# A fused attention and MLP kernel: its first six chunks of q loaded two tokens to a row, its first 420 operations put in a written order, its end cut over two PSUM banks

## The chip, the core and the metric

The kernel runs on one core of one Trainium2 chip. The metric is the device time of one execution in microseconds (us). Three runs of the kernel before the change took 611.60, 611.12 and 610.27 us; their median is 611.12 us. Engine names are those of the profile: PE is TensorE's matmul side and PEld its weight loads, DVE is VectorE, ACT is ScalarE, POOL is GpSimd, SP is SyncE, which here only issues DMAs. Times "at 37.9" are microseconds from the first instruction of the profiled execution.

## The reference

q, k and v have 4 batches, 8 heads, 768 tokens and a head size of 64. Tokens come in blocks of 64. For each batch and head:

```python
for b in range(nb):
    intra = einsum('bhic,bhjc->bhij', qb, kb) * Dmask         # lam ** (i - j), causal
    intra = einsum('bhij,bhjd->bhid', intra, vb)
    inter = einsum('bhid,bhde->bhie', qb * lam_pow, kv_state)
    out[:, :, sl] = intra + inter
    kv_state = lam_block * kv_state + einsum('bhsd,bhse->bhde', kb * rev_pow, vb)
x = out.transpose(0, 2, 1, 3).reshape(3072, 512)              # tokens x (heads, head size)
h = x @ w_in                                                  # 512 x 2048, float64 weights
return maximum(0.01 * h, h) @ w_out                           # 2048 x 512
```

The weights arrive as 64-bit floats and are turned into 32-bit ones on the chip.

## The kernel before

**Tiling.** A chunk `c` is 128 tokens (two blocks) of one batch, all heads; there are 24 chunks, six to a batch. Four chunks make a group `g` of 512 tokens, so there are six groups. `w_in` and `w_out` are cut into eight parts `p` of 256 hidden columns.

**Precision.** Each operand of the MLP is split in three tiles h, l and m (`xh`, `xl`, `xm` and `wh`, `wl`, `wm`), and a product is three passes of TensorE, h·h, l·l and m·m, in one PSUM bank, with one ACT rescaling (L658) ahead of the m pass.

**A chunk** goes through these steps. `load_kq` (L338) and `load_v` (L388) issue its loads on SP's queue: k and q in two halves of four heads, 128 KB each, v in one piece of 256 KB, all in rows of 64 floats. `transposes` (PE, L403) turns k and q by four 128x128 transposes each; ACT copies the results to SBUF (L414, L415); POOL or DVE scales k in place (L419) and makes the scaled q, `qsT` (L423; DVE for chunks 0 to 3, POOL after that). `scores` (PE, matmuls of 64x64 by `quad`, L313) makes the scores and the state's update, both in the bank `psc`. DVE masks the scores (L452) and adds the update to the state (L457, L459), POOL scales the state (L462). `outputs` (PE, L313) adds the masked scores times v and then, in two halves, the state's part in the bank `po`; between the halves a tiny copy (L491) is waited for. ACT makes `xh` (L507), DVE `xl` (L508) and `xm` (L510). Attention of a chunk needs the state of the chunk before it in the same batch.

**A weight part** `wi` takes two loads of 512 KB in rows of 2 KB (L566), three ACT operations for each half (L578, L580, L582), two DVE operations for each half (L584, L585) and then `wh` (ACT L591 or DVE L593), `wl` (DVE L596) and `wm` (DVE L602).

**Up** (`up(g, p)`, L640) multiplies a weight part with one group: for each of two halves f, four matmuls each of h, l and m, in one of three banks; ACT rescales and applies the leaky ReLU (L658, L661), and SP writes the result to DRAM (L664). From the third group on, **down** reads it back, splits it and multiplies it with `w_out` (L700) into eight accumulators, two for each of four blocks of 128 tokens: one for h and l, one for m.

**Order.** The kernel first records all its operations in a `Plan`, each with its engine (or two to choose from), a cost in us, what it reads and writes, and a rank from its place in the list `seq`. `emit` simulates the engines with these costs, always takes the operation that can start first, and then issues them engine by engine in the order found. Each engine executes its instructions in that order. Where the plan sees PE idle before the first product of the MLP, it puts in dummy transposes of the identity (`busy`, L266); nine more stand at the start (`WARM`).

**The end.** For the last block of 128 tokens, the m passes of the last two parts come last, in two halves of 256 columns of one accumulator in the bank `pt`; each half is then combined by DVE (L729) and written out on SP's queue (L732). After the last operation, PE runs 24 dummy matmuls of strips of the array and eight small ones (`strips`, L802, L809), whose results nobody reads.

## Time and profile before

| what | value |
|---|---|
| runs | 611.60, 611.12, 610.27 us; median 611.12 |
| profiled execution | span 609.73 us from first to last instruction; no other time is listed for it, and the median of the runs is 1.39 us above the span |
| busy | PE 601.4 us (99%), DVE 313.1 (51%), ACT 269.2 (44%), POOL 86.7 (14%) |
| mean granted TensorE clock | 1.000 |
| PE busy in stretches of 5 us from 0 to 40 | 3.14, 4.96, 3.81, 4.25, 3.51, 4.11, 4.53, 4.66 |
| PE busy from 40 to 600 | 559.6 of 560 |
| DVE busy from 15 to 40 | 22.8 of 25 |
| DMA | 105.18 MB, mean 173 GB/s; 180 to 295 GB/s in stretches of 1.5 to 7 us from 2.5 to 30 us |

The profile's page gives busy time as a share of the whole span. Here that says little, because the kernel has stages with different limits: the stretch up to 40 us, in which the loads, the first chunks and the first weights come in, and the rest. A group's "mean ns" is the length of one instruction from start to end; back to back, DVE's operations start 0.08 us closer than that, and PE's matmuls of 512 columns 0.226 us apart, because they overlap in the pipeline.

### The profile page before, as it was taken

To read this page: it belongs to the slowest core of one execution; us is meant where nothing else is said; L and a number is where in the kernel's file an instruction comes from. 1 tells how busy PE (TensorE), PEld (TensorE's weight loads), DVE (VectorE), ACT (ScalarE), POOL (GpSimd) and SP (SyncE) were. 2 spreads that over 40 slices of the span, in tenths; PEclk is the share of its full clock that TensorE was granted. 3 is DMA by queue.
4 is the path that set the end of the run, shared out by engine and by line. 5 is a ranking of instruction groups with operands and counts; after the bars stand their busy time and mean duration, and the time that the engine had idled before them with its cause. 6 is when DMAs were issued, how large, how long until landed. Compare 5 with 4: busy or idle time off the path is not lost.

```text
span 609.7 us, 13012 instructions
## 1 busy us (share of the span) xinstructions
PE 601.4 (99%) x5426; PEld 497.8 (82%) x5426; DVE 313.1 (51%) x418; ACT 269.2 (44%) x430; POOL 86.7 (14%) x90
## 2 busy tenths in 40 slices
PE   7799999999999999999999999999999999999999
PEld 6678888888888888888788888888888888888887
DVE  4999764334244426226366755545454544636531
ACT  4678974444465656555577522222222313214111
POOL 1654422114233004104000000000000000000000
DMA  9899865666888878887685843524334343333201
GB/s 208 219 267 249 239 190 136 167 150 186 190 219 240 217 229 215 214 245 214 226 304 218 284 145 103 173 71 142 133 104 137 108 135 114 130 104 125 82 1 69
DMA packets 147754, 105.18 MB, mean 173 GB/s; under 512 B 123632, under 2 KB 124400, under 8 KB 147696
## 3 DMA queue, kind: packets, MB, share of 16 engines
q1 hardware_dynamic: 147552, 104.36, 58.7%
q8 instruction: 42, 0.69, 0.5%
q14 instruction: 16, 0.13, 0.1%
q10 hardware_dynamic: 144, 0.00, 0.0%
HBM read 68.69 MB, written 35.65 MB: 171 GB/s over the span
## 4 chain that ended last, share of the span: by engine, by line
PE 95%; DVE 4%; DMA 1%; ACT 0%; issue 0%; DVEq 0%; ACTq 0%
PE b L640 43%; PE b L700 18%; PE po L700 11%; PE psc L700 11%; PE po L313 4%; PE pt L700 4%; PE psc L313 4%; DVE w L585 1%; PE pt L403 1%; DMA att<-in_k_dram 1%; DVE w L584 0%; DVE att L452 0%; PE psc L802 0%; DVE att L459 0%; DVE att L423 0%; DVE wm L602 0%
## 5 line engine op out<-in xcount | busy, mean ns | idle before, releaser
L682 ACT ACTIVATE xh<-att 128x1024 fp32r<-128x1024 f32 x48 | 50.8, 1061 | 148.8 <-PE b L700 140.7
L683 DVE SCALAR_TENSOR_TENSOR xl<-att,xh 128x1024 fp32r<-128x1024 f32 x48 | 58.6, 1222 | 97.9 <-ACT xh L682 94.7
L640 PE MATMUL b<-xh,wh 128*128 128x512 f32 (+2 forms) x392 | 103.6, 387 | 1.2 <-ACT xh L507 0.8
L640 PE MATMUL b<-xm,wm 128*128 128x512 f32 (+2 forms) x392 | 104.4, 392 | 0.0
L640 PE MATMUL b<-xl,wl 128*128 128x512 f32 (+2 forms) x392 | 103.3, 387 | 0.0
L640 PEld LDWEIGHTS b<-xh,wh 128*128 128x128 f32 x392 | 72.9, 188 | 16.8 <-ACT xh L507 0.9
L640 PEld LDWEIGHTS b<-xl,wl 128*128 128x128 f32 x392 | 72.8, 188 | 14.8
L640 PEld LDWEIGHTS b<-xm,wm 128*128 128x128 f32 x392 | 71.4, 188 | 15.1 <-ACT b L658 0.3
L658 ACT ACTIVATE b<-b 128x512 f32<-128x512 f32 (+2 forms) x97 | 56.2, 580 | 60.5 <-PE b L640 60.3
L661 ACT ACTIVATE gs<-b 128x512 f32<-128x512 f32 (+2 forms) x97 | 56.9, 593 | 43.6 <-PE b L640 38.5
L700 PE MATMUL b<-wh,xh 128*128 128x512 f32 x192 | 74.7, 389 | 0.0
L700 PE MATMUL b<-wl,xl 128*128 128x512 f32 x192 | 74.7, 389 | 0.0
L685 DVE SCALAR_TENSOR_TENSOR xm<-xl,xh 128x1024 fp32r<-128x1024 f32 x48 | 58.7, 1225 | 4.7
L462 POOL TENSOR_TENSOR att<-att 128x256 f32<-128x256 f32 x40 | 35.0, 876 | 57.6 <-DVE att L459 57.6
L700 PEld LDWEIGHTS b<-wh,xh 128*128 128x128 f32 x192 | 36.0, 188 | 7.5
L700 PEld LDWEIGHTS b<-wl,xl 128*128 128x128 f32 x192 | 36.0, 187 | 7.4
L452 DVE TENSOR_TENSOR att<-psc,att 128x512 f32<-128x512 f32 x24 | 16.5, 689 | 42.6 <-PE psc L313 42.5
L423 POOL TENSOR_TENSOR att<-att 128x512 f32<-128x512 f32 (+1 forms) x20 | 24.5, 1223 | 95.5 <-DVE att L383 46.6
L700 PE MATMUL psc<-wh,xh 128*128 128x512 f32 x96 | 37.3, 389 | 0.0
L700 PE MATMUL psc<-wl,xl 128*128 128x512 f32 x96 | 37.3, 389 | 0.0
L700 PE MATMUL psc<-wm,xm 128*128 128x512 f32 x96 | 37.3, 389 | 0.0
L700 PE MATMUL po<-wh,xh 128*128 128x512 f32 x96 | 37.3, 389 | 0.0
(79 smaller groups left out, 793.0 us busy)
## 6 DMA issues: line engine op xcount, KB each, us to landing
att<-g SPq DMA_DIRECT2D x48, 512.0 KB, 3.3
g<-gs SPq DMA_DIRECT2D x47, 512.0 KB, 4.0
raw<-in_moe_w_in_dram SPq DMA_DIRECT2D x16, 512.0 KB, 5.6
raw<-in_moe_w_out_dram SPq DMA_DIRECT2D x16, 512.0 KB, 5.0
att<-in_k_dram SPq DMA_DIRECT2D x48, 128.0 KB, 4.2
att<-in_v_dram SPq DMA_DIRECT2D x24, 256.0 KB, 4.6
out_dram<-gs SPq DMA_DIRECT2D x23, 256.0 KB, 2.2
wo<-w SPq DMA_DIRECT2D x8, 512.0 KB, 5.9
```

The costliest lines, as they stand in the source:

```text
L313: nc.tensor.matmul(dst[HALF[cols]], lhsT=lhsT[HALF[rows]], rhs=rhs[HALF[rows]], start=start, stop=True, skip_group_check=True)
L403: nc.tensor.transpose(out=at[y], in_=src[:, 2 * y:2 * y + 2, :].rearrange("p a d -> p (a d)"), identity=ident)
L423: add(eng, us, lambda: e.tensor_tensor(o, x, _bc(pow_q, 2, 2)[:, :, m, :], op=ALU.mult), ["fq", dep], [f"qsT{i}"])
L452: add("DVE", 0.69, lambda: nc.vector.tensor_tensor(sc, psc[:, :, lower, :], decay, op=ALU.mult), ["psc", "fk"], ["sc"])
L462: add("POOL", 0.7, lambda new=new, j=j: nc.gpsimd.tensor_tensor(state[(j + 1) % 4], new, _bc(lam_c, 2, D), op=ALU.mult), [f"st{j % 4}", "f ...
L640: nc.tensor.matmul(dst, lhsT=w[z][:, kk * 2 * P + f * P:kk * 2 * P + (f + 1) * P], rhs=x[z][:, kk, toks], start=start and kk == 0, stop=kk ...
L658: add("ACT", ns, lambda b=b: nc.scalar.activation(out=b, in_=b, func=AF.Copy, bias=0.0, scale=S + 1.0), [], [kb], rank=-1.5)
L661: add("ACT", ns, lambda b=b, r=r: nc.scalar.activation(out=r, in_=b, func=AF.Prelu, bias=0.0, scale=1.0 / WS, alpha=0.01), [kb], [f"gs{jg} ...
L682: add("ACT", 1.05, lambda: nc.scalar.activation(out=h, in_=graw[j], func=AF.Copy, bias=0.0, scale=NEAR), reads, wr("h"))
L683: add("DVE", 1.25, lambda: nc.vector.scalar_tensor_tensor(l, graw[j], 1.0, h.bitcast(F32), op0=ALU.mult, op1=ALU.subtract), reads + [f"rh{ ...
L685: add("DVE", 1.25, lambda: nc.vector.scalar_tensor_tensor(m, l.bitcast(F32), -S, h.bitcast(F32), op0=ALU.mult, op1=ALU.add), [f"rh{j}", f" ...
L700: nc.tensor.matmul(acc[tb][z // 2][:, cols], lhsT=ring[j][z][:, f * T + tb * P:f * T + (tb + 1) * P], rhs=W[pp][z][:, f * d_model:(f + 1) ...
```

## The change

The change has these parts.

1. **Pairs.** For chunks 0 to 5, q is loaded for two chunks at once: partition p gets tokens 2p and 2p+1, so that a row in DRAM is 512 bytes, in two DMAs of 256 KB (`load_pair`, L457). One chunk's tokens then lie on 64 partitions, even and odd ones beside each other, and are turned by 16 matmuls of 64x64 with the identity (`go_pair`, L416) in place of four transposes. The copies put the tokens back in order, and the scaled q is made in two DVE operations, one for each block of 64 tokens (`scale_pair`, L609; one alone for the first chunk of a batch).
2. **Listed order.** `ORDER` names the first 420 operations and the engine of each; `emit` takes them in this order and plans only the rest itself. The list also sets the order of the loads on SP's queue. Buffers (`Slot`: PSUM banks `pt`, `b10`, `b11`, `b2`, raw and low tiles, output tiles) are given out in the order of the program instead of in turn. The MLP's first product is cut into two halves of 256 tokens, `("up", 0, 1, 0, 2), ("up", 0, 1, 2, 4)`, and the first can run once two chunks are through. k, v of chunks 2 and 3 and a pair of q go into tiles that are still free (`spot`, `pair`).
3. **Apart.** For chunks 0 to 3 the state's update goes to banks of its own (`pu_apart`) and not to `psc`; the scaled q is made by DVE for chunks 0 to 7 (`QS = 8`), and k may be scaled by DVE for these too (`KM = 8`).
4. **Planner.** Costs and delays are other numbers; operations can be marked so that the planner keeps DVE's and POOL's from overlapping (`lock`); dummy transposes at the start are 11 instead of nine.
5. **End.** The last m passes are cut at column 384. The first 384 columns stay in `pt`, the last 128 go to the second half of `psc`; the second piece is written out on ACT's queue. In these 128 columns of the last block, the m products of the last two parts are added onto what the first block has left in that bank, and those of the first six parts stay in `pt` unread. The dummy matmuls after the end (`strips`) are gone.

```diff
@@ Plan.emit
+        listed = {i for i, _ in self.order}
+        deps = self.resolve([i for i, _ in self.order] + [i for i in range(n) if i not in listed])
...
+        for i, e in self.order:
+            take(max(free[e], since(i, e)), i, e)
         while len(done) < n:
@@
-    WARM = 9
+    WARM = 11
-    KT, EARLY = "b11", 2
-    QS = 4
-    KM = 2
+    ORDER = [(int(x[:-1]), ENGINE[x[-1]]) for x in (
+        "3d 6t 4d 8s 7t 9s 29t 12t 26d 5d 96d 28t 30s 0v 2v 1v 10g 14v 31s 11v 19t 13t 15v 35t 16g 97s 37v 33v 32g 20t 21s 22t 98s 49d 50d 53t 52t 23s 99s 17v "
...
+    APART = 4
+    PAIRS = {"q": {0, 1, 2}, "k": set()}
+    QS = 8
+    KM = 8
@@
+    def load_pair(nm, c):
+        b, n, i = of(c)
+        y, (dst, keys) = (q if nm == "q" else k)[b, :, n * C:(n + 2) * C, :], pair(nm, c)
+
+        def go():
+            for z in range(2):
+                nc.sync.dma_start(out=dst[:, z * HP:(z + 1) * HP].rearrange("p h s d -> p h (s d)"),
+                                  in_=y[z::2].rearrange("h (p s) d -> p h (s d)", s=2))
+        move(1.75, go, [], keys, issue=1.0, name=f"{nm}{c}")
@@ transposes
+        def go_pair(nm, at):
+            rows, src = HALF[c % 2], pair(nm, c)[0]
+            for y in range(HP):
+                for s in range(2):
+                    for a in range(2):
+                        quad(at[y][:, s * C2:(s + 1) * C2], c % 2, src[:, 2 * y + a, s, :], ident[:, rows], a, start=y == 0 and s == 0)
...
+                def scale_pair(t):
+                    o = joined(qsTs[i][:, :, tokens(t)])
+                    x = apart(zq())[:, :, :, t * C4:(t + 1) * C4]
+                    nc.vector.tensor_tensor(o, x, joined(pow_q), op=ALU.mult)
@@ scores
+        apart = c < APART
+        kp = [Slot("bank") for _ in range(n_pu)] if apart else ["psc"] * n_pu
-        add("PE", 0.47, kv, [f"k{i}", f"v{i}"], ["psc"])
+        add("PE", 0.47, kv, [kk, kv_], kp, kind="q")
@@ down
-            halves = [slice(0, d_model // 2), slice(d_model // 2, d_model)]
+            cut = [slice(0, 3 * P), slice(3 * P, d_model)]
+            ends = [(acc[tb][1], ACC[tb][1]), (acc[0][1], ACC[0][1])]
...
+                    queue = nc.scalar if i else nc.sync
@@
-    seq = [("a", 0), ("a", 1), ("a", 2), ("a", 3), ("wi", 1), ("b", 4), ("r", 4), ("up", 0, 1), ("wi", 0), ("r", 5),
+    seq = [("a", 0), ("a", 1), ("a", 2), ("a", 3), ("wi", 1), ("b", 4), ("r", 4), ("up", 0, 1, 0, 2), ("up", 0, 1, 2, 4), ("wi", 0), ("r", 5),
@@ after plan.emit()
-    strips(2, 6)
-    strips(4, 3)
-    f = graw[0]
-    for _ in range(4):
-        for i in range(2):
-            nc.tensor.matmul(spare[2][HALF[i], 0:C2], lhsT=f[:, 0:C2], rhs=f[:, 0:C2], start=True, stop=True, skip_group_check=True)
```

In the built program, SP's queue now begins: k of chunk 0, the pair q 0 and 1, k 1, v 0, the first half of weight part 1, k 2, the pair q 2 and 3, v 1, the second half of part 1, v 2, k 3, the first half of part 0, v 3, its second half, the pair q 4 and 5, k 4, k 5, v 4, the two halves of part 2, v 5. Before, it began: k 0, q 0, v 0, k 1, q 1, v 1, the first half of part 1, q 2, k 2, its second half, v 2, q 3, k 3, q 4, v 3, the first half of part 0, k 4, q 5, v 4, its second half, k 5, q 6, v 5, q 7, the two halves of part 2. On PE, the state's update of chunk 3 now stands between the two halves of the state's part of chunk 2, and the first products of the MLP follow behind chunk 2, ahead of chunk 3's `outputs`; before, the first product came behind chunk 3.

## The prediction, made before the changed kernel ran

> **What bounds the kernel now.** I read the page first: its busy times, then the 40 slices.
>
> ```profile
> PE 601.4 (99%) x5426; PEld 497.8 (82%) x5426; DVE 313.1 (51%) x418; ACT 269.2 (44%) x430; POOL 86.7 (14%) x90
> ...
> PE   7799999999999999999999999999999999999999
> ```
>
> PE is busy all the time but in the first slices, and busy there is not useful: dummies (L266) count. The windows put a border at 40 us: PE is busy 559.64 of 560 us from 40 to 600, and 32.97 before 40. So whatever PE is given earlier in the start comes out at the end, as long as nothing starves it later. The timeline of PE then gives the mark that I use.
>
> ```profile
> 24.67 1.16 PE L313 MATMUL psc<-att 64*64 64x64 f32 x64 [1.31 <-DVE xl L508]
> 25.76 0.77 PE L266 MATMUL b<-att 128*128 128x128 f32 x5
> 26.64 0.93 PE L313 MATMUL po<-att 64*64 64x64 f32 x48
> ...
> 29.39 2.11 PE L640 MATMUL b<-xh,wh 128*128 128x512 f32 x8 [0.78 <-ACT xh L507]
> ...
> 35.93 2.12 PE L640 MATMUL b<-xm,wm 128*128 128x512 f32 x8
> 37.88 1.08 PE L640 MATMUL b<-xh,wh 128*128 128x512 f32 x4
> 39.30 0.98 PE L640 MATMUL b<-xh,wh 128*128 128x512 f32 x3 [0.34 <-ACT gs L661]
> ```
>
> The first MLP product starts at 29.39, behind chunk 3. The second weight part (part 0) starts at 37.88: call this the mark. By then PE has done chunks 0 to 3, part 1 with group 0, the transposes of chunks 4 and 5 and the scores of 4. In the changed order the same work stands ahead of that product, except four m matmuls of 256 columns. What set the mark is DVE, which the chain of waits follows for most of 10 to 39 us:
>
> ```profile
> 27.43 1.64 DVE L596 SCALAR_TENSOR_TENSOR wl<-wh,w 128x1024 fp32r<-128x1024 f32 x1
> 29.32 1.98 DVE L602 SCALAR_TENSOR_TENSOR wm<-wl,wh 128x1024 fp32r<-128x1024 f32 x1
> ...
> 33.01 1.43 DVE L585 CUSTOM_DVE_ANT_0 w<-w,low 128x1024 uint16<-128x1024 uint16 x1
> ...
> 35.64 1.43 DVE L593 TENSOR_SCALAR wh<-w 128x1024 fp32r<-128x1024 f32 x1
> ```
>
> These forms take 1.22, 1.22, 0.69 and 0.69 where POOL is idle. From 15 to 40, such excesses on L584, L585, L593, L596, L602 add up to 4.4 us against 14.94 us of POOL: 0.3 us for each us of POOL. DVE was fed late as well: by the landing events, v of chunk 3 arrived at 24.54, part 0's halves at 26.0 and 31.43.
>
> The end, by the timeline of the last 10 us:
>
> ```profile
> 604.62 1.11 PE L700 MATMUL pt<-wm,xm 128*128 128x256 f32 x8
> 605.83 0.76 DVE L729 SCALAR_TENSOR_TENSOR gs<-pt,raw 128x256 f32<-128x256 f32 x2 [1.72 <-PE pt L700]
> ...
> 608.14 0.69 PE L809 MATMUL po<-att 128*64 128x64 f32 x16
> ```
>
> The two DVE halves start only after both PE halves. The last output lands at 608.465 by its event; the last dummy ends at 608.85, and SP's closing wait lasts until then.
>
> **The change part by part. Loads.** In the trace's packet records a 256-byte packet takes 18.7 ns, one of 2 KB 97 ns, one of 512 bytes 27.1 ns (256 of these, all writes). On 16 engines a load of 256 KB in 256-byte rows is 64 packets each, 1.20 us; 512 KB in 2 KB rows 1.6; half a pair of q 32 x 27.1 = 0.87. The ends for the last, as reads of 512 bytes are not in the trace: 0.78 (pace of 2 KB rows) and 1.20 (no gain); I take 0.87, the same size of packet. The first half of k lands at 4.00, so bytes flow from 3.4. Ahead of and with v of chunk 3 the new order has eight loads of k and v (9.6), four half pairs (3.5) and three weight halves (4.8): 17.9, so v lands near 21.5 with 0.2 of slack, 3 us earlier. The ends are 21.1 and 22.8. SP may keep eight loads in flight, and I see no wait on a buffer that holds a load up past its turn. Part 0's second half then lands at 23.1 (-8.3), the pair 4 and 5 at 24.8, k of 4 at 26.0.
>
> [...]
>
> **Chunks 0 to 2.** The new order makes chunk 1 wait for v 1, which lands near 14.5 instead of 10.25 (two pairs and k 2 are ahead of it); before, chunk 1's outputs stood at 16.14 anyway. The banks of its own for the state's update take away the waits of `psc` on L459 and L508 (1.8 and 1.3 us in the waits). I cost both at nothing more: chunk 3's update is behind v 3 at 21.5. Even at the old spacing of 5 us, outputs from 15.0 are through chunk 2's first half by 21.
>
> **From 21.5 to the mark, on PE.** State's update of chunk 3 0.47, second half of chunk 2 0.4 (22.4); xh 0.6, xl 0.7, beside three products of 256 columns (0.49 each, between 0.40 for 128 and 0.69 for 384), so chunk 3's outputs start at 23.8 and end at 25.2 (0.93 and a half, with the tiny copy between). ACT has four weight conversions (0.67 to 0.78) ahead of chunk 3's xh, which comes at 27.0; PE fills this with q 4 and 5 (0.88) and one product, and idles. Then six products of 256 columns and a last m (3.4), k 4 and 5 (0.88), update and scores of chunk 4 (0.94): 32.3. The two halves instead of one group cost 12 x 0.49 - 6 x 0.91 = 0.42 and are in this.
>
> **On DVE.** It waits for xh of chunk 3 at 27.0 too; then stand an xl, two xm, a k, two adds (L585's kind) and `wh`, 7 x 0.61 back to back, and two shifts, 2 x 0.34: 4.95, so `wh` of part 0 is there at 31.9. Beside it POOL has four state scalings (0.62) and one k (1.06), 3.5 us, so 1.0 of excess: 32.9. The ends are 0 and 3.5. The mark is at 32.9, 5.0 earlier; less 0.49 of m matmuls left over: 4.5 gained.
>
> **After the mark.** Before, PE had 15.5 us of work to the first m product of part 2 (53.75), while DVE was through with its `wm` at 49.7: 3.7 of cover. `QS = 8` adds 2.7 us to DVE (two of 0.41 for chunks 4 and 5, 0.41 and 0.69 for 6 and 7) and takes 5.1 us off POOL, worth 1.4: net 1.3, inside that cover. Close to the mark the cover is thin: `wm` of part 0 comes 5.5 us behind its `wh`, and PE has 6.1 us until it needs it. I put 0.3 of new idle there (ends 0 and 2).
>
> Edits with one answer: a pair's 16 matmuls are priced between a quarter of 64 (0.29) and twice that, as they use half of the quadrants at once; I take 0.44, what the four transposes take, so nothing. Copies with a stride (0.59, at most 0.78 as L580) lie on ACT ahead of DVE, but for q 4 and 5 in its idle time. Eleven dummies for nine end at 4.0, where the first load lands: nothing.
>
> **The end.** Four matmuls of 384 columns (0.174 each) and four of 128 (0.105) take 1.12 against 0.95; the first piece goes to DVE at 605.6 (0.55), lands 1.9 behind that, as before plus 0.2 for its size: 608.06. The second, from 606.05 for 0.27, has its own queue and lands by 608.1. That is 0.35 earlier, and without dummies SP's wait ends there: 0.4 more. 0.75.
>
> **Sum.** 4.5 - 0.3 + 0.75 = 5.0 of a span of 609.73, so 604.8; the median of the runs is 1.39 above the profiled span, 611.12, which gives 606.1.
>
> **Rivals.** *The start gains little.* Half pairs at 1.20 (v 3 1.3 later) and 3.5 of excess put the mark at 36.7: 0.7 gained there and 0.75 at the end, 609.7. The excess alone puts it at 35.4: 608.7. So 608.1 to 609.9. For it: DVE was 22.8 of 25 busy; against: POOL loses work.
>
> *More is gained.* No excess, no idle behind the mark, and chunk 3's xh ahead of ACT's conversions: below 604.4. For it: from 4 to 38 PE idles 4.8 us (7.03 up to 40, less 2.2 outside) and runs 21 dummies of 0.2; against: loads alone hold chunk 3 to 21.
>
> *Slower: PE falls to its slow pace.* The start shows two paces: 32 small matmuls took 1.13 at 7.28 and 0.69 at 9.07, four transposes 1.28 at 4.04 and 0.66 at 9.70, while the granted clock reads 1.00. Dummies are now planned only up to the first MLP product, and PE waits around v 3 and xh 3. At the slow pace (1.6 to 1.9 times) the 11 us of work from 21 to 33 cost 7 to 10 more: 613 to 616. It decides once more than 6 to 8 us of work run slow. Against: waits of 1.07 and 1.31 left the matmuls behind them at 1.16 for 64. [...]
>
> *Not what it says.* The end could gain nothing, were the pieces still combined together: 606.8. The built program has separate waits for them, so that is small.
>
> **How the numbers follow.** Runs of this kernel spread by 0.2%, 1.2 us: that is about what a measurement can tell from no change. My forecast, 604.4 to 608.1 (the sum with one unknown at an end), 0.58; little gained, 608.1 to 609.9, 0.17; more gained, 0.10; within 0.2%, 0.04; slower, by the pace or a wait that I don't see, 0.11. So faster 0.85. The range 603.2 to 609.6 takes in most of the second and of the third case.
>
> **What would show it.** Landing of v 3 near 21.5; the first MLP product by 23 and part 0's by 33 in PE's timeline; L585, L593, L596, L602 near 0.69 and 1.22; no idle of PE behind 40; the last output at 608.1 less the gain. Wrong it is if PE's rows of 256 columns take 0.9 instead of 0.49, or if windows behind 40 show idle of more than 1 us.

## The result and the profile after

The changed kernel takes 615.00 us (median of 8 runs, 609.91 to 616.68) where the kernel before, run beside it, takes 611.26 (8 runs, 610.27 to 612.38). The ratio is 1.0041 with a 95% interval of 1.0024 to 1.0058: slower by 0.4%, where 0.8% faster was forecast. The profile was taken of the fastest of the eight executions, 609.91 us with a span of 608.12. It shows the change at its best, and has to be read together with a profile of one of the others.

First the page of the changed kernel, its line of busy times and two rows of the 40 slices:

```profile
PE 601.1 (99%) x5569; PEld 501.5 (82%) x5569; DVE 309.8 (51%) x428; ACT 265.1 (44%) x430; POOL 74.5 (12%) x85
...
PE   9899999999999999999999999999999999999997
...
PEclk9999999999999999999999999999999999999999
```

TensorE is as busy as before and issues 143 matmuls more (5569 against 5426). Then PE's timeline up to the mark (start, length, engine, line, operation, count, and in brackets the idle time ahead with its releaser):

```profile
9.81 1.11 PE L550 MATMUL b<-att 128*128 128x128 f32 x4
...
23.63 0.22 PE L416 MATMUL pt<-gs 64*64 64x64 f32 x1
...
24.48 0.73 PE L864 MATMUL b<-xh,wh 128*128 128x256 f32 x4
25.52 0.75 PE L864 MATMUL b<-xl,wl 128*128 128x256 f32 x4 [0.31 <-DVE wl L822]
27.27 0.74 PE L864 MATMUL b<-xh,wh 128*128 128x256 f32 x4 [1.00 <-issue]
27.94 0.69 PE L416 MATMUL po<-att,gs 64*64 64x64 f32 x32
...
33.52 0.64 PE L864 MATMUL b<-xl,wl 128*128 128x256 f32 x4
...
37.60 1.08 PE L864 MATMUL b<-xh,wh 128*128 128x512 f32 x4
```

The mark, part 0's first product, stands at 37.60: 0.28 us earlier than before and 4.7 later than the forecast 32.9. Chunk 3's outputs start at 27.94, not at 23.8. Ahead of them stands a wait of 1.00 us that the profile puts down to nothing ("issue"). PE was late before that: the state's update of chunk 3, forecast for 21.5, starts at 23.63, although v of chunk 3 landed at 20.95.

The clock row says 9 from the first slice on, but this run's clock records begin at 13.69, and the page counts what lies ahead of them as full. The rows say otherwise: the four transposes at 9.81 take 1.11 us, four such transposes at 16.18 take 0.66 (shown further below), and 32 small matmuls at 12.83 take 1.03 where such 32 take 0.70 at 22.88. So this run, too, started at a slow pace.

What the change did for the other engines came as forecast. DVE's costly forms between 15 and 40 us (behind the count: busy us and mean ns of one instruction, then idle us ahead):

```profile
L811 DVE CUSTOM_DVE_ANT_0 w<-w,low 128x1024 uint16<-128x1024 uint16 x4 | 2.8, 699 | 0.1
L822 DVE SCALAR_TENSOR_TENSOR wl<-wh,w 128x1024 fp32r<-128x1024 f32 x2 | 2.4, 1220 | 0.0
...
L819 DVE TENSOR_SCALAR wh<-w 128x1024 fp32r<-128x1024 f32 x1 | 0.7, 694 | 0.0
```

They had taken 999, 1426 and 1430 ns in the same stretch before. The end, in the timeline of the last microseconds, from the m products of the last block on:

```profile
603.46 0.87 PE L931 MATMUL pt<-wm,xm 128*128 128x384 f32 x4
604.17 0.56 PE L931 MATMUL psc<-wm,xm 128*128 128x128 f32 x4
604.42 0.56 DVE L963 SCALAR_TENSOR_TENSOR gs<-pt,raw 128x384 f32<-128x384 f32 x1 [1.48 <-PE pt L931]
604.90 0.28 DVE L963 SCALAR_TENSOR_TENSOR gs<-psc,raw 128x128 f32<-128x128 f32 x1
605.21 0.36 ACTq L966 DMA_DIRECT2D out_dram<-gs  x1
```

From the start of these m products (604.62 before, 603.46 after) to the end of the span it is 5.11 us before and 4.66 after: 0.45 gained, where 0.75 was forecast.

The other seven runs are 2.6 to 6.8 us slower than this one, and their mean granted TensorE clock is 0.988 to 0.997 instead of 1.000. Two differences are to be explained: this one, and the 3.8 us by which the fastest run itself lies above the forecast.

### The profile page after: what moved, and what is told of

Same layout as the page of the kernel before. It is cut to its first block, busy times and chain, and to the rows that moved or that the text cites. A ratio compares the mean times of both kernels' runs of the same rounds, so it can differ in the third digit from the quotient of the medians.

```text
span 608.1 us, 13275 instructions
## 1 busy us (share of the span) xinstructions
PE 601.1 (99%) x5569; PEld 501.5 (82%) x5569; DVE 309.8 (51%) x428; ACT 265.1 (44%) x430; POOL 74.5 (12%) x85
## 4 chain that ended last, share of the span: by engine, by line
PE 98%; issue 1%; DVE 1%; POOL 0%; ACT 0%; DVEq 0%; POOLq 0%
PE b L864 33%; PE b L931 18%; PE pt L864 11%; PE po L931 11%; PE psc L931 11%; PE po L416 4%; PE pt L931 4%; PE psc L416 3%; PE b L416 1%; PE b L550 1%; PE b L355 1%; PE po L550 0%; PE pt L416 0%; DVE att L648 0%; POOL att L658 0%
## 5 line engine op out<-in xcount | busy, mean ns | idle before, releaser
L864 PE MATMUL b<-xm,wm 128*128 128x512 f32 (+3 forms) x300 | 78.2, 385 | 0.0
L864 PE MATMUL b<-xh,wh 128*128 128x512 f32 (+3 forms) x300 | 77.2, 380 | 1.0 <-issue 1.0
L864 PE MATMUL b<-xl,wl 128*128 128x512 f32 (+3 forms) x300 | 77.3, 381 | 0.3 <-DVE wl L822 0.3
L864 PEld LDWEIGHTS b<-xh,wh 128*128 128x128 f32 x300 | 54.8, 188 | 11.7 <-issue 1.2
L864 PEld LDWEIGHTS b<-xl,wl 128*128 128x128 f32 x300 | 54.8, 188 | 11.1 <-DVE wl L822 0.5
L864 PEld LDWEIGHTS b<-xm,wm 128*128 128x128 f32 x300 | 53.9, 188 | 10.6
L892 ACT ACTIVATE gs<-b 128x512 f32<-128x512 f32 (+1 forms) x72 | 42.2, 589 | 38.1 <-PE b L864 37.7
L931 PE MATMUL psc<-wm,xm 128*128 128x512 f32 (+1 forms) x100 | 37.9, 384 | 0.0
L931 PE MATMUL po<-wm,xm 128*128 128x512 f32 x96 | 37.4, 389 | 0.0
L931 PE MATMUL po<-wl,xl 128*128 128x512 f32 x96 | 37.3, 389 | 0.0
```

Of the source, the lines that this page charges most:

```text
L864: nc.tensor.matmul(dst, lhsT=w[z][:, kk * 2 * P + f * P:kk * 2 * P + (f + 1) * P], rhs=x[z][:, kk, toks], start=start and kk == 0, stop=kk ...
L892: add("ACT", ns, lambda b=b, r=r: nc.scalar.activation(out=r(), in_=b(), func=AF.Prelu, bias=0.0, scale=1.0 / WS, alpha=0.01), [kb], [kg], ...
L931: nc.tensor.matmul((to if z == 2 else acc[tb][0])[:, cols], lhsT=ring[j][z][:, f * T + tb * P:f * T + (tb + 1) * P], rhs=W[pp][z][:, f * d ...
```

## First runs: the clock, the end, or the order

Three theories were set against each other: R (the clock is released late or taken back at the start), T (the filling products that were removed from the end matter), O (the order itself is slower). Four kernels ran beside the kernel before (612.19 us, 23 runs).

The changed kernel once more:

> The changed kernel as it is. Theory R (release): TensorE starts at half pace and is released at a moment that differs from run to run; in the changed kernel this comes late (the first profile's clock record starts at 13.69 us), because the start has mostly 64x64 matmuls and small gaps. Then the times spread over 609 to 617, the clock record of this profile starts anywhere from 9 to 25, and the later it starts, the longer the span. Theory T (tail): the dummy matmuls at the end, which the change took away, left TensorE in a faster state for what follows. This run does not tell the two apart; it shows whether a second profile has the same start. Theory O (order): the listed order alone loses the time (second half of part 0 issued at 21.65), at any pace; then the times agree within 1 us and the start looks as in the first profile.

Measured 615.16 us (10 runs, 610.95 to 617.48), ratio 1.0041 (1.0015 to 1.0067). Its profiled execution is one of the longer ones, 615.57 us. The clock row of its page has two reduced slices, the first and the third, of 15.3 us each:

```profile
PEclk8979999999999999999999999999999999999999
```

PE's timeline of this run from the first product on, and the windows that follow (columns: window, its length, busy time of PE, PEld, DVE, ACT and POOL with instruction counts, granted clock, DMA share, GB/s):

```profile
24.91 0.73 PE L864 MATMUL b<-xh,wh 128*128 128x256 f32 x4
25.95 0.74 PE L864 MATMUL b<-xl,wl 128*128 128x256 f32 x4 [0.30 <-DVE wl L822]
29.05 1.22 PE L864 MATMUL b<-xh,wh 128*128 128x256 f32 x4 [2.37 <-issue]
...
36.74 1.05 PE L864 MATMUL b<-xh,wh 128*128 128x256 f32 x4
...
39.09 0.64 PE L864 MATMUL b<-xl,wl 128*128 128x256 f32 x4
...
43.15 1.08 PE L864 MATMUL b<-xh,wh 128*128 128x512 f32 x4
```

```profile
25.14:28.56 3.42, 1.25 (x8) 0.84 (x7) 3.42 (x7) 2.24 (x5) 1.62 (x2) 1.00 1.17 258
28.56:31.97 3.41, 2.71 (x52) 2.30 (x52) 1.08 (x2) 0.14 (x2) 0.54 (x1) 0.50 0.79 190
31.97:35.38 3.41, 3.33 (x78) 3.33 (x79) 1.62 (x3) 1.31 (x3) 0.00 (x0) 0.50 0.55 163
35.38:38.80 3.42, 3.42 (x22) 3.30 (x21) 0.11 (x1) 1.23 (x3) 0.00 (x0) 0.50 0.49 128
```

The wait without a releaser is 2.37 us here. It leaves PE busy for 1.25 of 3.42 us, and in the next three windows the clock is granted at one half. The same four matmuls of 256 columns take 1.05 to 1.22 us there and 0.64 to 0.75 at full clock. The mark comes at 43.15, 5.55 later than in the fastest run; behind it the two profiles agree (570.6 and 570.5 us).

The two profiles are of the same kernel, so the 5.55 us can be divided. The first product is 0.43 later, the wait at the third product 1.37 longer. From this third product to the first product behind the half clock it is 6.25 us in the fastest run (27.27 to 33.52) and 10.04 here (29.05 to 39.09): 3.8 us go to the half clock.

Theory R had the release of the clock come late in the longer runs. It is the other way round here: the clock records begin at 4.67 in this run and at 13.69 in the fastest. What is left of R is that the clock is taken back. Theory O, by itself, had the times agree within 1 us; they spread over 6.5.

The filling products at the end put back, and taken away from the kernel before:

```diff
+    strips(2, 6)          # changed kernel: again after plan.emit(), with the eight small ones
+    strips(4, 3)
```

> The changed kernel with the dummy matmuls of the end put back. Theory T: the start is fast again and the time falls to 607 or less, with no clock record of half pace. Theories R and O: as the changed kernel, 610 to 617, with at most 0.4 us more for the end.

Measured 617.56 us (8 runs), ratio 1.0088 (1.0063 to 1.0114).

```diff
-    strips(2, 6)          # kernel before: none of the 32 filling products at the end
-    strips(4, 3)
```

> The kernel before without the dummy matmuls of the end. Theory T: slower by 2 to 6 us and a wide spread. Theories R and O: 0 to 0.4 us faster, spread as before (610 to 612).

Measured 611.72 us (10 runs), ratio 1.0000 (0.9985 to 1.0014). Theory T falls: the filling products at the end help neither kernel. Why the changed kernel is 2.4 us slower with them stays open. Its profile shows the wait at the third product again (2.65 us), and half clock from 31.7 to 41.9. But two of its eight runs took 613.85 and 614.92 us at a mean clock of 1.000, so a clock that is taken back is not all of the loss.

More warming up:

```diff
-    WARM = 11
+    WARM = 40
```

> The changed kernel with 40 instead of 11 dummy transposes at its start, some 7 us more of whole-array work before the first real transposes. Theory R: the release comes by 9 us, the spread of the times shrinks to 2 us and the median falls to 606 to 611 although the first transposes start 3 to 5 us later. Theories T and O: the start is only later, 3 to 5 us slower than the changed kernel, and the spread stays.

Measured 616.04 us (4 runs), ratio 1.0075 (1.0047 to 1.0103), where theory R expected 606 to 611. The clock is better (mean 0.996), but 29 more transposes at the start are 29 more to get through ahead of the first chunk, and the mark is at 39.29 with a clock of 1.00 from 4.88 on.

**Reading the clock of every run.** In the clock records of these profiles half rate lasts a whole number of windows of 3.41 us: in the repeated run one from 8.08 to 11.49 and three from 28.56 to 38.80. The last stretch is the exception, which in the fastest run begins at 607.61, behind PE's last work, and is 2.55 us long. One window lowers the mean clock of a run by 3.41/2/610 = 0.0028, so the mean clock counts them. It does so roughly: it leaves out what lies ahead of the first record (which begins between 4.3 and 6.2 us in 15 of the 17 profiles with clock records, at 10.55 and 13.69 in the other two; the profile of the kernel before has none), and it takes in that last stretch. For the 18 runs of the changed kernel in two sets:

```
windows at half clock   runs   us
0                       1      609.91
1                       2      610.95, 614.95
2                       7      612.14 to 615.79, median 612.65
3                       3      614.75 to 617.34
4                       5      615.05 to 617.48
```

A line through them gives 611.0 us without any and 1.37 us for each (correlation 0.75). The price includes the waits that go ahead of such windows. The kernel before has one such window in 2 of 23 runs here and in 7 of 33 in the next set, and never two.

## Second runs: fill the gap, empty the gap, free the queue, the end alone

The theories now: G (idle time at the waits lets the clock fall, and that is the loss), L (work and loads are late, the clock costs nothing itself), S (a blocked queue delays the start). The kernel before took 611.92 us beside them (33 runs).

Two long products in place of short fillers:

```diff
+    FILL = {7: 2, 157: 2}     # ahead of q's first quarters and of part 1's first product
+        nc.tensor.matmul(bank[at].rearrange("p (x t) -> p x t", x=4), lhsT=ident, rhs=_bc(ident, 1, 4), ...)
```

> The changed kernel with TensorE kept busy in its two emptiest places: the three filling transposes before q's first quarters become two long products of 128x128 by 512 columns (about 0.9 us each), and two more of them stand before the first product of part 1. They cost TensorE up to 1.8 us where it would not have waited, and they bring no data earlier. Theory G (the loss is the clock: two windows of 3.41 us in which TensorE is busy for 0.60 and 0.36 or less, each followed by one or three windows at half clock): the mean granted clock rises from 0.988-0.994 to 0.997-1.0 in most runs and the median falls by some 2 to 4 us, to 611-613 us. Theory L (the loss is the late start alone, loads and instructions that come late; the clock falls because of it and costs nothing itself): no gain or a loss by the added work, 615-617 us, whatever the clock does.

Measured 613.30 us (11 runs, 611.95 to 616.68), ratio 1.0035 (1.0017 to 1.0053), which cannot be told from the changed kernel's 1.0041 and lies between the ranges of G and L; mean clock 0.995 against 0.992 to 0.993. The wait at the third product is gone in the profile. Instead there is one of 2.44 us earlier, with half clock behind it:

```profile
14.55 0.27 PE L428 MATMUL po<-att 64*64 64x64 f32 x1 [2.44 <-issue]
```

So the fillers neither won the expected 2 to 4 us nor lost anything by their 2 to 3 us of work. The wait is not bound to the product. It moves. Theory L, too, has the repeated run against it, where rows of the same form took 1.05 to 1.22 us at the half clock and 0.64 to 0.75 at full clock, more than a half longer.

The kernel before without the fillers in its gaps:

```diff
-    plan.idle, plan.spare, plan.warm = busy, "b10", 1.3 + 0.22 * WARM
+    plan.idle, plan.spare, plan.warm = None, "b10", 1.3 + 0.22 * WARM
```

> The kernel before, with the 13 filling transposes that it puts into TensorE's gaps between 5 and 27 us left out (the 9 at the very start stay). Nothing else moves, the data come as before. Theory G: TensorE's busy share of some windows of 3.41 us falls from 0.63-0.89 to 0.4-0.6, half clock follows in at least one place before 38 us, the mean granted clock is 0.988-0.997 and the time 613-616 us. Theory L: the gaps stay gaps, 611-612 us.

Measured 612.28 us (10 runs), ratio 1.0012 (1.0001 to 1.0022). The half clock came as theory G said, in 7 of 10 runs and up to three windows; its price was far below the expected 2 to 5 us. Where its slow windows fell is not shown: the run that was profiled, 610.76 us, is not one of the seven.

The blocked load moved back in the list:

```diff
-  ... 70s 181d 183s 182s 176s 112d ... 111d 121d 113d ...
+  ... 70s 176s 112d ... 111d 121d 181d 183s 182s 113d ...
```

> The changed kernel with one load (the second half of part 0 of the input weights, with its two ScalarE reads) moved in the listed order from ahead of the pair q 4/5 to behind the loads of k4 and k5. It writes the buffer of the pair q 2/3, and SyncE's queue stood still for that buffer from about 16.5 to 21.65 us. Theory S (the blocked queue delays the start): the DMA share from 20 to 25 us rises from 0.48 to 0.8 or more, the pair q 4/5 lands at 23-25 us in place of 27.4, the outputs of chunk 3 and the first product of part 0 come 0.5 to 2 us earlier, the time falls by 0.5-2 us. Theory G: the loads come earlier, but the wait of TensorE at its third product of part 1 (1.0-2.6 us, no data missing) stays, and with it the half clock in most runs: mean clock 0.988-0.994, within 1 us of 615.

Measured 614.10 us (11 runs), ratio 1.0042 (1.0017 to 1.0067): no change. Yet the loads did what was asked. The window from 20 to 25 us, first of the changed kernel, then of this one:

```profile
20.00:25.00 5.00, 5.00 (x201) 4.62 (x201) 4.48 (x9) 4.00 (x8) 2.82 (x4) 1.00 0.48 149
```

```profile
20.00:25.00 5.00, 3.27 (x115) 2.82 (x118) 3.25 (x8) 3.35 (x5) 2.73 (x4) 1.00 0.96 237
```

The DMA share doubles from 0.48 to 0.96 and the pair q 4/5 lands at 24.8 instead of 28.3, but PE stands still more often: four waits without a releaser, 6.4 us together, against 3.5 in the repeated run. Theory S falls as far as the time goes: freeing the queue won nothing. Whether the earlier loads were worth something that the longer waits took away is not shown.

The end alone, on the kernel before:

```diff
+            cut = [slice(0, 3 * P), slice(3 * P, d_model)]
+                    queue = nc.scalar if i else nc.sync
-    strips(2, 6) ...
```

> The kernel before with only the end of the change: m products of the last block in 384 and 128 columns into two banks, the second output on ScalarE's queue, the filling products at the end gone; the start is that of before. All theories that hold the start responsible: 0.6-0.8 us less than before, 610.4-610.8 us where before has 611.2, mean clock as before. If the end is what is slow: 612 us or more.

Measured 610.96 us (11 runs), ratio 0.9991 (0.9981 to 1.0000). That is 1.0 us by the medians and 0.6 by the ratio, whose interval reaches from nothing to 1.2: the forecast 0.75 lies in it. So the loss lies in the start.

## What PE waits for

In the changed kernel, repeated, and in variants told of below these waits stand at fixed counts of PE's matmuls, whatever operation stands there. "Count" is the number of matmuls that PE has executed from the start, where each 64x64 fp32 product is two (a chunk's transposition, 16 products by the code, is 32 records):

```
count   unchanged, repeated   fillers (c1)       upper half (d1)    junk (d2)          list empty (d3)
223     -                     outputs, chunk 0   -                  -                  scores
350     outputs, chunk 1      -                  -                  -                  -
477     outputs, chunk 2      -                  outputs, chunk 2   update, chunk 2    -
605     third product         -                  outputs, chunk 3   -                  quarters
```

The counts are 127 or 128 apart. The page lists as many weight loads as matmuls (5569 each), so 128 matmuls with theirs are 256 instructions. In the DMA records of the trace, the queue named "instruction" moves packets of 16 KB, 43 of them in an execution with 11,138 instructions of PE, which is 43.5 times 256; divided evenly, a packet has 64 bytes for each of 256 instructions. Over 19 profiled executions there are 35 waits of more than 0.25 us within two matmuls of these counts (or of the next, 733) between 5 and 50 us. Among them are all 32 of that stretch that the profile puts down to nothing; the other three have a load or another engine as their releaser. In 33 of them PE starts again 1.25 to 1.64 us after a 16 KB packet has ended; in the repeated run of the changed kernel the packet of count 605 runs from 26.46 to 27.65 and PE goes on at 29.05. From the queue's name, the packets' size and their times I infer that PE waits there for its own code; which engine's instructions a packet holds is not on record.

The packets that start between 15 and 29 us in the fastest profile do so when PE has executed 258, 400, 601 and 657 matmuls: if they bring the blocks that begin at 350, 477, 605 and 733, each of the four starts when PE is inside the block before its own. Matmuls 478 to 605 start between 22.41 and 25.99 there, the packet runs from 24.95 to 25.95, and PE goes on at 27.27. So, on this reading, PE came to the end of its 128 matmuls before the next block was there. How late the packet starts differs for the same code: from matmul 477 to the packet's start it is 2.54 us in the fastest profile and 3.50 in the repeated one, where the waits are 1.00 and 2.37. What sets this delay is open; that the loads on the other queues hold the packets up is a rival that no run was made for. The kernel before has the same waits, but smaller (0 in the profile that was shown, 0.42, 0.55 and 2.0 us in three variants of it).

Idle time of PE, whatever its cause, also goes ahead of the falls of the clock. In the 17 profiles with clock records, cut into the clock's own windows of 3.41 us, full clock turned into half 16 times up to 600 us. All 12 windows with PE busy for 0.58 or less were followed by half clock; of 13 between 0.59 and 0.65, three were; of all the others one (0.82). In nine of these 16 windows most of the idle time is a wait at one of the counts above, in the other seven it is waits for loads of q or v. Full clock came back only behind a window that was busy for 0.99 or more, and in four cases one such window was not enough. A window with two fifths of idle time was enough in the repeated run: from 4.66 to 8.08 PE is busy for 2.05 of 3.42 us, idle in pieces of 1.04 and 0.33 us, and from 8.08 to 11.49 the clock is granted at one half.

## Third runs: fewer and more matmuls, without list, without pairs

Theory F: the blocks of code set the waits. Rival D: the waits belong to the work at these places. The kernel before took 612.02 us beside them (17 runs).

```diff
-  quad(at[y][...], c % 2, src[:, 2 * y + a, s, :], ident[:, rows], a, ...)
+  nc.tensor.matmul(at[y][HALF[a], ...], lhsT=upper_half(src[rows, 2 * y + a, s, :]), rhs=upper_half(ident[rows, rows]), ...)
```

> The changed kernel, with the quarters of q's pairs transposed from the upper 16 bits alone: q of the first six chunks is cut to bfloat16. What it leaves out is the lower half of these values, so its output is not exact; loads, buffers, order and all else stay. A quarter is then one pass (one weight load and one matmul) in place of two, so each of the six transpositions of a pair issues 16 matmuls and not 32, 96 fewer up to 30 us. Theory F (TensorE's own instructions come in blocks of 128 matmuls, 16 KB, fetched only after the block ahead has been entered; the waits without a releaser stand at matmul 223, 350, 477, 605 of every run, where a block begins, and the idle time there lets the clock fall): the waits stay at these counts, but the counts are reached further on in the work, so they get shorter and fewer, the mean clock rises to 0.994-1.0 and the median falls by 1.5 to 5 us, to 610-613.5 us. Rival D (the waits belong to the work at these places, to data or buffers): the waits stay with the operations where they are now, that is 64 matmuls earlier by count at the third product of part 1, and the time stays within 1 us of 615 us.

Measured 610.22 us (12 runs, 607.95 to 612.43), ratio 0.9976 (0.9962 to 0.9990): 4.9 us less than the changed kernel, and faster than the kernel before. The waits stayed at their counts and met other operations:

```profile
29.23 0.27 PE L416 MATMUL po<-att 64*64 64x64 f32 x2 [1.12 <-issue]
```

That is count 605 again, now in chunk 3's outputs, behind the third product. This decides between F and D as to where the waits are. It does not give their price alone, because the transposition itself got shorter. A pair's quarters in the changed kernel, the four whole transposes behind them, and the quarters from the upper half:

```profile
15.10 1.15 PE L416 MATMUL b<-att,raw 64*64 64x64 f32 x32
16.18 0.66 PE L550 MATMUL pt<-att,gs 128*128 128x128 f32 x4
16.77 0.69 PE L416 MATMUL b<-att 64*64 64x64 f32 x32
```

```profile
20.70 0.42 PE L560 MATMUL b<-att,raw 64*64 64x64 bf16 x16
21.05 0.66 PE L550 MATMUL b<-att,gs 128*128 128x128 f32 x4
```

From start to start the quarters take 1.08 us, the four transposes 0.59, the one-pass quarters 0.35. The scores or the update, also 32 matmuls of 64x64, take 0.51: by the code, all the quarters of a chunk read the same half of the rows and the others alternate between both. That this is the reason is not shown by a run of its own.

```diff
+            for x in range(8):
+                quad(at[0][:, 0:8], c % 2, ident[:, 0:C2], ident[:, 0:8], x % 2, start=True)
```

> The changed kernel with 8 more small products (64x64 by 8 columns, two passes each, so 16 matmuls) ahead of each transposition of a pair, written to where the transposition then writes: 96 more matmuls up to 30 us, about 0.2 to 0.4 us of TensorE's time for each of the six. Theory F: the blocks run out earlier, the waits without a releaser at 223, 350, 477, 605 get longer, more windows at half clock, the time rises by 1 to 4 us to 616-619 us. Rival D: only the work added, and part of it in gaps: 615-616 us, with the half clock as often as before.

Measured 616.71 us (6 runs), ratio 1.0081 (1.0058 to 1.0103): 1.6 us more than the changed kernel. The added products take 0.48 us a time, 2.9 in all, so work alone could explain it. What the run does show is the place again, count 478, now in the state's update of chunk 2:

```profile
23.70 0.27 PE L416 MATMUL b<-gs 64*64 64x64 f32 x1 [2.78 <-issue]
```

The list and the pairs:

```diff
-    plan.idle, plan.warm, plan.order = busy, 1.3 + 0.22 * WARM, ORDER
+    plan.idle, plan.warm, plan.order = busy, 1.3 + 0.22 * WARM, []
```

> The changed kernel with the listed order empty, so that the planner orders all operations; the pairs, the new end and all else stay. If the listed order is what costs: 610-612 us. If the pairs with their fourfold number of small products cost, whatever the order (theory F): 614-618 us with a mean clock under 0.997.

Measured 619.19 us (6 runs), ratio 1.0117 (1.0087 to 1.0147), mean clock 0.995: above both ranges.

```diff
-    PAIRS = {"q": {0, 1, 2}, "k": set()}     # and the list empty, as above
+    PAIRS = {"q": set(), "k": set()}
```

> The changed kernel with the listed order empty and no pairs: q comes by chunks and is transposed by 4 whole transposes, in the planner's order; the new end, the banks and the filling rule of the changed kernel stay. Theory F: with 144 matmuls fewer ahead of 40 us the waits without a releaser are as in the kernel before, the mean clock is 0.997 or more, the time 610-613 us. If it is neither pairs nor order but the buffers and banks of the rest: 614 us or more.

Measured 617.94 us (5 runs), ratio 1.0113 (1.0096 to 1.0131), and that with a mean clock of 0.997. The expectation on theory F was wrong: without the list the rest of the change (banks, buffers, the planner's new costs) is slow by itself, with or without pairs; the mark is at 42.1 in this profile. The list is no loss, it repairs the rest. What the pairs cost can only be seen inside it.

## Fourth runs: the pairs taken out of the list

In the list each pair's load was replaced by the loads of its two chunks at the same place, its quarters by four transposes, its two scalings by one. The kernel before took 612.17 us (29 runs).

```diff
-    PAIRS = {"q": {0, 1, 2}, "k": set()}
+    PAIRS = {"q": set(), "k": set()}         # e1;   {1, 2} in e2,   {0} in e3
-  "3d 6t 4d 8s 7t 9s 29t 12t 26d 5d 96d 28t ...
+  "3d 6t 4d 27d 8s 7t 9s 30t 12t 26d 5d 95d 29t ...
```

> The changed kernel with its listed order, but q of all chunks loaded by chunks and transposed by 4 whole transposes: in the list each pair's load becomes the two loads of its chunks at the same place, each transposition by quarters becomes one by 4 transposes, each pair of scalings by halves one scaling. TensorE issues 28 matmuls fewer for each of six transpositions, 168 up to 30 us, 112 of them ahead of the products of part 1; the rows of q fall from 512 to 256 bytes, which by the packets' times (2 x 18.7 against 27.1 ns) costs the DMA engines some 0.17 us for each chunk, 1 us in all. Theory F (instruction supply): waits without a releaser up to 40 us under 1 us in all, mean clock 0.997-1.0, time 608.5-611.5 us. Theory P (the list needs the pairs' faster loads; what costs is data that come late): 613-617 us.

Measured 611.69 us (12 runs), ratio 0.9996 (0.9985 to 1.0006), mean clock 0.997: 3.5 us less than the changed kernel, and the intervals are apart. In its profile the mark stands at 37.17, but PE idles for 1.85 us between 40 and 600 (0.28 in the changed kernel): a part of what the start gains is lost behind it.

> As the changed kernel, but the first pair alone (q of chunks 0 and 1) is loaded by chunks and transposed whole; pairs 2/3 and 4/5 stay. 56 matmuls fewer, all of them ahead of matmul 130. Theory F: between the changed kernel and the one without pairs, 610-614 us, mean clock about 0.994-0.997; the first wait at matmul 223 moves further on in the work. Theory P: 614-617 us.

Measured 611.38 us (12 runs), ratio 0.9995 (0.9981 to 1.0008), mean clock 0.995.

> As the changed kernel, but only q of chunks 0 and 1 as a pair; chunks 2 to 5 are loaded by chunks and transposed whole. 112 matmuls fewer, 56 of them ahead of the products of part 1. Theory F: 609.5-613 us, nearer to the kernel without pairs, mean clock about 0.997. Theory P: 613-616 us.

Measured 611.99 us (12 runs), ratio 0.9993 (0.9979 to 1.0007), mean clock 0.997.

Theory P falls: the slower rows of q cost nothing that shows, and the pairs are what costs. Each of the three reaches the level of the kernel before; they cannot be told apart, and taking out the first pair alone gave as much as taking out all. So the price is not the same for each pair; why all three together cost it is not shown. Nor is the sum of the waits for code the price: in the profile with one pair they come to 3.6 us, as in the repeated changed kernel (3.5), and this run took 612.01 us with two windows at half clock against 615.57 with four.

Last, the long fillers at the blocks where code was waited for:

```diff
+    FILL = {42: 1, 59: 1}     # list without pairs;   {53: 1, 90: 1} with pairs 2/3 and 4/5
```

> The changed kernel's listed order without pairs, and one long product (128x128 by 512 columns, two passes, 0.9 us) put in TensorE's queue just ahead of each of the two blocks of its code for which it waited longest (the block that begins at matmul 223 and that at 350). Theory F with the clock: the fetch goes on while the long product runs, so its 0.9 us are mostly taken out of the wait; the windows that held 0.39 of busy time hold 0.6 or more, half clock is seen in fewer runs (mean clock 0.998-1.0 against 0.997), the time falls by 0.3 to 1.2 us to 610.5-611.4 us. Rival: the long products only add their 1.8 us where the wait did not come: 612-613.5 us.

Measured 610.92 us (12 runs), ratio 0.9986 (0.9974 to 0.9998).

> The changed kernel's listed order with pairs 2/3 and 4/5 alone, and two such long products: ahead of the first transposition by quarters (in place of the short filling transposes there; TensorE waited 1.1 us for the pair's load) and ahead of the block at matmul 605. Theory F with the clock: mean clock from 0.995 to 0.998 or more, time 610-611 us, 0.4 to 1.4 us less than without them. Rival: 612-613 us.

Measured 610.97 us (12 runs), ratio 0.9992 (0.9980 to 1.0004).

The kernel before took 611.61 us beside them (23 runs). For the list without pairs the answer on the clock is clear: without the fillers 11 of 12 runs had half clock, with them 2 of 12 (mean clock 0.997 and 0.999). On the time it is not: 0.9986 and 0.9996 overlap. With two pairs the fillers did not do it: half clock in 7 of 12 runs after 9 of 12, mean clock 0.997 where 0.998 or more was expected, and the time cannot be told from that without fillers. With the list, without pairs, with the new end and two long fillers the kernel is 0.14% faster than the kernel before, the fastest here that keeps all of q; the new end alone is 0.09% faster, and the two cannot be told apart.

## Why the prediction was wrong, step by step

**The price of a pair: mis-sized, outside both its ends.** "A pair's 16 matmuls are priced between a quarter of 64 (0.29) and twice that ... I take 0.44 ... so nothing." The 64 rows from which this was scaled are the records of 32 products: in the records an fp32 product of 64x64 is two (32 for a chunk's 16 products, and 16 where they are bf16). A chunk's transposition is 32 records and takes 1.08 us, 0.5 more than the four transposes; by the prediction's own rule, with the records counted right, it would have been 0.58 to 1.16. Four of them lie ahead of the update of chunk 3, which is 2.1 us late, and two between chunk 3's outputs and the mark: 3 us on an engine that is busy for all of 5 to 15 and 20 to 25 us. With the waits of 0.31 and 1.00 that comes to 4.3 of the 4.7 us by which the mark is late in the fastest run; this sum is worked out from one profile and not shown by a run.

**PE's code: not in the sum at all.** The wait without a releaser is 1.0 us in the best profile and 3.5 in the repeated one. The trace before gave a hint only in the queue of instruction packets, 42 of 16 KB. No term, no rival and no "what would show it" looked there.

**The slower rival: given too small a chance.** It got 0.11 together with other waits, and against it stood waits of 1.07 and 1.31 us, behind which 64 matmuls had still taken 1.16. The repeated run has 2.17 us of idle in the window from 25.14, most of it the wait for code, which the forecast did not have, and three windows at half clock behind it. What the rival describes did happen, products of 256 columns at 0.86 from start to start among it, one of the forecast's own signs of being wrong. Its condition ("once more than 6 to 8 us of work run slow") was just met, by rows that take 6.25 us at full clock; they cost 3.8 us, where the rival had 11 us of work and 7 to 10 us. So it is partly luck that its time, 613 to 616, holds the measured 615.0: it put the whole loss down to the pace, and a part of it has the two causes above.

**"I see no wait on a buffer that holds a load up past its turn": wrong, without effect.** Part 0's second half went into the buffer of the pair q 2/3, and SP's queue stood until the last quarters had read it: issued at 21.65, landed at 25.47 (forecast 23.1), and behind it the pair 4/5 at 28.3 (24.8) and k of 4 at 29.1 (26.0). Moving it won nothing.

**What held.** v of chunk 3 landed at 20.95 (21.5); a packet of 512 bytes took 30.0 ns (27.1), which makes 0.96 us for half a pair (0.87); DVE's excess went; products of 256 columns follow each other at 0.48 at full clock (0.49); idle from 40 to 600 us is 0.28 after 0.36. The end gave 0.45 of the 0.75 in the profile: the second piece lands 3.65 us behind the first m product and not 3.48, and the program closes 1.0 us behind that landing where it had closed 0.9 behind the last dummy. So loads and DVE were freed as forecast. PE, which the forecast let wait for them, had become the engine that set the mark.

Put together from runs of their own: the end is worth -1.0 us, the start without pairs +0.7 (611.69 against 610.96, not told from nothing), the pairs +3.5. By the ratios these are -0.6, +0.3 and +2.8. The sum, +3.2, is near the loss of the changed kernel (615.16 against 612.19) by construction, since each step is a difference of two of these kernels. Between two runs of the changed kernel the half clock made 3.8 of 5.55 us. How the pairs' 3.5 us divide among their longer transposition, the waits for code and the half clock stays open: each edit that changed one changed another too.

## What to carry to other kernels

Before adding small matmuls to a stretch, count the records that the trace shows for one call, and count the instructions: here the load with longer rows came with a transposition of 32 records in place of four. The two profiles of the changed kernel have 1.0 and 3.5 us of waits that I put down to PE's own code, where the listed order without pairs has none up to 45 us that the profile puts down to nothing. The sign was "issue" waits 127 or 128 matmuls apart. And when runs of one kernel differ by a few microseconds, look at the mean granted clock of each run first: here it counted the half-rate windows, and PE's busy share in the 3.41 us ahead of each tells which gaps went before it. Look at the rows as well, because the mean left out the slow start ahead of the first clock record.

## Not expected of the hardware

The queue "instruction" moved packets of 16 KB, 43 for 5569 matmuls with their weight loads; 37 of the 43 in the fastest profile took 0.88 to 1.29 us, and in 33 of 35 waits PE went on 1.25 to 1.64 us after one had ended. The clock fell to half behind all 12 windows of 3.41 us in which PE was busy for 0.58 or less and behind four others (0.59 to 0.65 and 0.82), and stayed there for one window (from 8.08 us) and for three (from 28.56) in the repeated run. In the fastest run 32 small matmuls at 12.83 us took 1.03 us, against 0.70 at 22.88, while the page showed the clock as full. In the same run sixteen 64x64 fp32 products that by the code all read the same half of the rows took 1.08 us (at 15.10), sixteen over both halves 0.51 (at 16.77).
